# A feed-forward or output tile beside attention: one group of sixteen score pairs instead of two groups of eight

## The chip, the cores and the metric

The kernel runs on one core of a Trainium2 chip. The metric is the device time of one execution in microseconds (us), of which less is better. Numbers for a stretch come from one profiled execution.

## What is computed

A transformer block on x of shape [1, 2048, 512] in float32: 32 heads of 16 for attention, a SwiGLU feed-forward layer of width 1792, and shifts, scales and gates from a condition vector c.

```python
mod = (silu(c) @ w_mod).reshape(c.shape[0], 6, 1, -1)
sa, ca, ga, sb, cb, gb = (mod[:, 0], ..., mod[:, 5])
h = layernorm(x) * (1 + ca) + sa
q, k, v = split(h @ wqkv)                       # 32 heads of 16
p = softmax(einsum("bhqd,bhkd->bhqk", q, k) * 16 ** -0.5)
x = x + ga * (merge(p @ v) @ wo)
h = layernorm(x) * (1 + cb) + sb
x = x + gb * ((silu(h @ w_gate) * (h @ w_up)) @ w_down)
```

## The kernel before

The 2048 queries are cut into four chunks of 512. Attention goes by **units**: 32 of them, each four heads of one chunk. A unit has 16 **steps**, one for each tile of 128 keys; a step has four **pairs**, one for each head. So there are 512 steps and 2048 pairs, and `done` counts pairs.

A pair is two matmuls on TensorE (PE), one in the upper and one in the lower half of the rows of its array, so that they run at the same time, each streaming 512 columns:
- the **score** (`score`, L571): keys by queries of one head, into one of the PSUM banks that `bank` hands out in turn. ScalarE (ACT) reads it and writes its exponential into a tile `pt` (L573).
- the **maximum** (`max_one`, L523): the scores of a unit 20 steps ahead, from whose row maxima the exponent's shift comes. VectorE (DVE) reduces it (L525). Its bank comes from `four`.

A score must wait until ACT has read the score that had its bank before; a maximum likewise for DVE.

The **value products** (`pv_step`, L586) multiply the exponentials of a step with the values. A half of a step is four matmuls, one for each head, in four column strips of the array, over all its 128 rows; float32, so each goes through twice, 256 columns each time. They may be made for steps that end 4 or more pairs before the last pair issued (`4 * halves[0][0] + 8 <= done`), so after each block of them four exponential tiles stay unread.

Attention of the next chunk runs together with the dense layers of the chunk that it has left. In `plain` sections it runs alone: windows of three pairs (`WIN`), then a few halves of value products; scores rotate through three banks (4, 5, 6). In `filled` groups eight pairs are interleaved with twelve **slots** of a dense tile, then come up to six halves of value products (four in the steady state). A slot is two matmuls with 64 of the tile's 128 contracted rows each, one in each half of the array, into the two banks of the tile (3 and 6, `FBANKS`). `accumulate` makes the 24 slots of a tile: phase 0 gives one output the upper and the other the lower rows, phase 1 swaps them. Maxima then have banks 0, 1, 2, scores only 4 and 5, and value products 7. How many slots follow each pair is a table:

```python
TWO = (0, 3, 2, 2, 2, 2, 1, 0)
DOWN = (0, 3, 3, 0, 3, 3, 0, 0)
```

A tile of the gate and up projections, or of the output projection, took two groups of `TWO`, so that a block of value products stood between its phases. A tile of the down projection has 12 slots in all, takes one group of `DOWN`, and changes phase inside the group (`trade=True`): an empty instruction on ACT waits for the last matmuls of phase 0, and the first ones of phase 1 wait for it, so that the row halves do not write a bank at the same time.

All engines' orders are written out by the program (`manual_schedule`); PE and ACT work through theirs in order. What a group has left to do for its tile (tanh, products, additions) is in `posts` and `behind`, what a unit has left (its denominators, `out_a` to `out_c`) in `due`. Row maxima are turned by `max_rows` with three small matmul forms on PE in `plain` sections and by `max_turned` with DVE and a small ACT instruction (L563) in `filled` ones.

Of the kernel before, what the change touches and what calls it, by code (L numbers as in the profile page):

```python
# [11 lines left out]
F32 = mybir.dt.float32  # L12
# [9 lines left out]
P = 128  # L22
# [8 lines left out]
CW = S // NC  # L31
# [8 lines left out]
LEAD = 21  # L40
# [2 lines left out]
HALVES = (2, 1, 1, 2)  # L43
ORDER = (0, 2, 1, 3)
UG = 16 * NG
PTS = 13
FBANKS = (3, 6)
KEEP = 7
REST = 24
NORM = 9  # L50
STARTS = (147, 275, 403)
TWO = (0, 3, 2, 2, 2, 2, 1, 0)
DOWN = (0, 3, 3, 0, 3, 3, 0, 0)
ALONE = {TWO: (0, 4, 0, 4, 0, 4, 0, 0), DOWN: (0, 6, 0, 0, 0, 6, 0, 0)}


# [5 lines left out]
def take(it, k):  # L62
    run(islice(it, k))
# [40 lines left out]
def block_kernel(ctx, tc, x, wqkv, wo, w_gate, w_up, w_down, c, w_mod, out):  # L104
    nc = tc.nc
# [23 lines left out]
    one = const.tile([P, 1], F32, name="one")  # L129
# [8 lines left out]
    o_dr = dram.tile([NC, NG, P, CW], F32, name="o_dr")  # L138
# [353 lines left out]
    pb = ctx.enter_context(tc.tile_pool(name="pb", bufs=2, reuse_waits="tile"))  # L492
    kop[1] = pb.tile([P, 2, S], F32R, name="kop1", bufs=1)
    pf = None
    qop, mx, pts, pv, o_, due, res = {}, {}, {}, {}, {}, {}, {}
    posts, behind = [], []
    n = 16 * NU
    last = NC - 1
# [66 lines left out]
    def score(i, h):  # L565
        u, kt = divmod(i, 16)
        rows = slice(64 * (h % 2), 64 * (h % 2) + KR + 2)
        p_ = pb.tile([P, CW], F32, name="pt_", tag="pt", bufs=PTS)
        pts.setdefault(i, {})[h] = p_
        sp = bank("st_")  # L570
        nc.tensor.matmul(sp, kop[u % 3][rows, h // 2, kt * P:(kt + 1) * P], qop[u][rows, h // 2, :],  # L571
                         start=True, stop=True)
        nc.scalar.activation(p_, sp, AF.Exp, scale=SCALE)  # L573
# [35 lines left out]

    def out_c(u, eng, mul, o, rb):  # L610
        ci, g = divmod(u, NG)
        on = pf.tile([P, CW], F32, name="on", tag="on", bufs=1)
        mul.tensor_mul(on, o, rb)  # L613
        eng.dma_start(o_dr[ci, g], on)

    def at(i, f):
        due.setdefault(i, []).append(f)
# [13 lines left out]
    def tile_mid():  # L631
        return pf.tile([P, 2, CW], F32R, name="mid", tag="mid", bufs=3)

    def tmp(name):
        return pf.tile([P, CW], F32, name=name, tag="tmp", bufs=4)
# [177 lines left out]
    def add_o(ch, t0, outs, late):  # L813
        if ch.mv is None:
            ch.mv = pf.tile([P, 4, 2], F32, name="mv2", tag="mv2", bufs=1)
            ch.rs = pf.tile([P, 4], F32, name="rs", tag="rs", bufs=1)
            ch.rs2 = pf.tile([P, 2, 4], F32, name="rs2", tag="rs2", bufs=1)
        for e in range(2):
            t = t0 + e
            nc.vector.tensor_add(ch.x2[:, t, :], outs[e], ch.x2[:, t, :])  # L820

        def sums(t):
            st = pf.tile([P, 6], F32, name="stt", tag="stt", bufs=2)
            nc.vector.bn_stats(st, ch.x2[:, t, :])
            nc.vector.bn_aggr(ch.mv[:, t, :], st)

        def minus_mean(t):
            nc.scalar.activation(tmp("sq"), ch.x2[:, t, :], AF.Identity, scale=-1.0 / D,
                                 accum_out=ch.mv[:, t, 0:1])

        def squares(t):
            nc.scalar.activation(tmp("sq"), ch.x2[:, t, :], AF.Square, bias=ch.mv[:, t, 0:1],  # L832
                                 accum_out=ch.mv[:, t, 1:2])

        if late:
            turns = (1, 2, 2, 3) if t0 == 0 else (1, 2, 3, 4)
            works = ((minus_mean, t0), (squares, t0), (minus_mean, t0 + 1), (squares, t0 + 1))
            behind.extend([k, lambda f=f, t=t: f(t)] for k, (f, t) in zip(turns, works))
        else:
            for e in range(2):  # L840
                sums(t0 + e)

    def out_pair(ch, t0, outs, halves):
        return accumulate(outs, lambda e, a, k: ch.oT[a][:, k, (t0 + e) * P:(t0 + e + 1) * P],
                          lambda b, k: ch.wo[k // 2][:, b, k % 2, :], NK,
                          lambda: posts.append(lambda: add_o(ch, t0, outs, True)), halves)

    def out_terms(ch, t, pt, ks):
        for k in ks:
# [1 line left out]
                nc.tensor.matmul(pt, ch.oT[a][:, k, t * P:(t + 1) * P], ch.wo[k // 2][:, b, k % 2, :],  # L851
                                 start=(k == 0 and a == b == 0), stop=(k == NK - 1 and a == 1))

    def gate_up(ch, f, outs, halves):
        ch.load_gu(f + ch.ahead)
        if f == 0:
            ch.load_wd(0)
        ch.mid[f] = mid = tile_mid()

        def after():  # L860
            th = tmp("th")
            nc.scalar.activation(th, outs[0], AF.Tanh, scale=0.5)  # L862

            def later():
                q = tmp("q")
                nc.vector.scalar_tensor_tensor(q, th, 1.0, outs[0], op0=ALU.add, op1=ALU.mult)  # L866
                m32 = tmp("m32")
                nc.vector.tensor_mul(m32, outs[1], q)  # L868
                slow = halves or (ch.ci, f) == (last - 1, NF - 2)
                (nc.gpsimd.tensor_copy if slow else nc.scalar.copy)(mid[:, 0, :], m32)  # L870
                (nc.gpsimd if slow else nc.vector).tensor_sub(mid[:, 1, :], m32, mid[:, 0, :].bitcast(F32))  # L871
            posts.append(later)

        w = ch.w.pop(f)
        return accumulate(outs, lambda e, a, k: w[:, 2 * e + a, k, :], lambda b, k: ch.hT[b][:, k, :], NK, after,
                          halves)

    def down(ch, m, t0, outs, halves):
        def later():
# [98 lines left out]
    halves = [(i, half) for i in range(n) for half in range(2)]  # L978
    done, ended, owed = 0, 0, 0
# [16 lines left out]
    for i in range(-LEAD, -1):  # L996
# [7 lines left out]
        if i == -2:  # L1004
            four, work = three, bank
# [11 lines left out]
    def pvs(most, by_halves):  # L1017

        nonlocal owed
        if by_halves:  # L1020
            most, owed = most + owed, 0
        while most and halves and 4 * halves[0][0] + 8 <= done:
            i, half = halves.pop(0)
            pv_step(i, half)
            most -= 1
            if i % 16 == 15 and half:
                close_unit(i // 16, done // 4 - 1)
                if by_halves:
                    break
        if by_halves and most and halves and 4 * halves[0][0] + 8 <= done:  # L1030
            owed = most

    def turns_behind():
        for b in list(behind):
            b[0] -= 1
            if not b[0]:
                b[1]()
                behind.remove(b)

    def end_steps():  # L1040
        nonlocal ended
        while ended < done // 4:
            after(ended - 1)
            ended += 1

    def plain(steps, tails=()):

        nonlocal four, bank, beside
        beside = False
        assert steps % WIN == 0 and done % 4 == 0  # L1050
        four, bank = Turn(0, 3, 1, 2), Turn(4, 5, 6)
        for w in range(4 * steps // WIN):
            for _ in range(WIN):
                pair_of()
            if w < len(tails) and tails[w]:
                tails[w](four())
            pvs((HALVES[(w - 2) % 4] if done > 8 else 0) + (w == 4 * steps // WIN - 1), True)
            turns_behind()
            end_steps()

    def filled(places, work):

        nonlocal four, bank, beside
        beside = True
        four, bank = three, Turn(4, 5)
        if done >= 4 * n - 4 * (LEAD - 1):
            places, bank = ALONE.get(places, places), Turn(4, 5, 0, 1, 2)
        for r in range(len(places)):
            pair_of()
            take(work, places[r])  # L1070
            if r % 4 == 3:
                end_steps()
        hook()
        pvs(6, False)
        turns_behind()

    def two_of(u):
        return [kop[u % 3][:, e, :].rearrange("p (k c) -> p k c", k=NK) for e in range(2)]
# [9 lines left out]
    outs = [banks[b] for b in FBANKS]  # L1088
    pvs(3, False)
    for ci in range(last):  # L1090
        plain(STARTS[ci] - done // 4)
        ch = chunks[ci]
        for t0 in (0, 2):
            work = out_pair(ch, t0, outs, True)
            filled(TWO, work)
            filled(TWO, work)
        behind.append([4, lambda: scaled(ch)])
        tails = [lambda tp, k=k: ch.turned(tp, k) for k in range(NK)]
        plain(NORM, [None] * NORM + tails[:3])
        plain(WIN, tails[3:])  # L1100
        if ci == last - 1:
            plain(REST)
        for _ in range(len(ch.jobs) - (KEEP if ci == last - 1 else 0)):
            job, args = ch.jobs.pop(0)
            if args == (NF // FG - 1, 0):
                plain(WIN)
            work = job(ch, *args, outs, True)
            for places in (TWO, TWO) if job is gate_up else (DOWN,):
                filled(places, work)
    chunks[last - 1].load_gu(NF - 2)  # L1110
    filled((0,) * 4, iter(()))

# [2 lines left out]
    turns = chain([2, 3, 2, 0, 1, 2, 0], cycle([1, 3, 2, 0]))  # L1115
# [19 lines left out]
    ch, chp = chunks[last], chunks[last - 1]  # L1135
# [4 lines left out]
    on = out_b(NU - 1, nc.scalar, *res[NU - 1])  # L1140
    on = out_r(NU - 1, nc.scalar, *on)
# [48 lines left out]
```

## Time and profile before

| | |
|---|---|
| median of 3 runs | 1829.33 us (1827.03 to 1829.35) |
| the profiled execution | 1826.86 us, of which its span 1825.0 us |
| PE matmuls busy | 1816.3 us (100% of the span) |
| PE weight loads busy | 1202.5 us (66%) |
| DVE busy | 1521.2 us (83%) |
| ACT busy | 1248.0 us (68%) |
| GpSimd (POOL) busy | 459.9 us (25%) |

Matmuls that run in different parts of the array overlap, and their ends are modelled, so PE's 100% says that it hardly ever stood with nothing issued, not that no time can be taken out. The start times of successive matmuls tell more than the busy time.

### The profile page before, as it was taken

The numbers are of one execution on the slowest core, as the hardware profiler recorded it, in microseconds if no ns is written. First come the engines' busy times: TensorE is split into PE (matmuls) and PEld (weight loads), VectorE is DVE, ScalarE is ACT, GpSimd is POOL, SyncE is SP. The second block draws the span as 40 slices with busy tenths as digits, with TensorE's granted clock in tenths as the row PEclk, the third lists the DMA queues.
The fourth block names the chain that finished last, engine by engine and source line by source line (L and its number), as shares of the span: only waits on it lengthen the run. The fifth ranks groups of instructions, "written<-read, shape, count | busy, mean of one in ns | idle before, by whom it ended". The sixth has DMA issues, their size and how long they took to land.

```text
span 1825.0 us, 40961 instructions
## 1 busy us (share of the span) xinstructions
PE 1816.3 (100%) x16904; PEld 1202.5 (66%) x16904; DVE 1521.2 (83%) x2554; ACT 1248.0 (68%) x2358; POOL 459.9 (25%) x538
## 2 busy tenths in 40 slices
PE   9999999999999999999999999999999999999999
PEld 7876444444465777776565777776564577777887
DVE  5578999999999888888999888889999988832544
ACT  4223888888888766777888767767888876673211
POOL 3612544556223111111123111111113011131200
PEclk9999999999999999999999999999999999999999
DMA  9883876667845444453544554444643536333742
GB/s 307 288 232 138 203 199 172 179 167 199 207 81 125 103 122 143 115 149 70 145 110 105 141 125 118 122 118 91 161 80 57 116 90 157 134 123 120 279 167 108
DMA packets 80486, 267.62 MB, mean 147 GB/s; under 512 B 19604, under 2 KB 24212, under 8 KB 59620
## 3 DMA queue, kind: packets, MB, share of 16 engines
q1 hardware_dynamic: 61324, 179.71, 34.0%
q0 software_dynamic: 18288, 84.49, 19.5%
q8 instruction: 133, 2.18, 0.5%
q10 hardware_dynamic: 688, 0.80, 0.1%
q14 instruction: 53, 0.43, 0.1%
HBM read 201.85 MB, written 62.13 MB: 145 GB/s over the span
## 4 chain that ended last, share of the span: by engine, by line
PE 83%; DVE 14%; ACT 1%; DMA 0%; issue 0%; SPq 0%; DVEq 0%
PE bank L586 21%; PE bank L789 20%; PE bank L571 14%; DVE mx L525 14%; PE bank L523 11%; PE bank L808 8%; PE bank L213 7%; PE bank L851 1%; PE bank L772 0%; DMA wm_ab<-in_w_mod 0%; PE bank L165 0%; ACT sq L832 0%; DVE v_flat L882 0%; PE bank L537 0%; SPq L261 0%
## 5 line engine op out<-in xcount | busy, mean ns | idle before, releaser
L525 DVE TENSOR_REDUCE mx<-bank 128x1 f32<-128x512 f32 x2048 | 1273.3, 681 | 111.0 <-PE bank L523 63.7
L571 PE MATMUL bank<-qop,kop 50*128 50x512 f32 x2048 | 729.7, 426 | 0.4 <-ACT pt__16494 L573 0.2
L523 PE MATMUL bank<-kop,qop 48*128 48x512 f32 x2048 | 724.6, 425 | 0.3
L571 PEld LDWEIGHTS bank<-qop,kop 50*128 50x128 f32 x2048 | 343.1, 184 | 168.9 <-issue 49.8
L523 PEld LDWEIGHTS bank<-kop,qop 48*128 48x128 f32 x2048 | 342.8, 184 | 106.2 <-DVE mx L525 62.1
L789 PE MATMUL bank<-act,wgu 64*128 64x512 f32 x1872 | 303.5, 392 | 0.0
L789 PEld LDWEIGHTS bank<-act,wgu 64*128 64x128 f32 x1872 | 199.4, 187 | 22.5
L613 POOL TENSOR_TENSOR on<-o,rb 128x512 f32<-128x512 f32 x31 | 39.9, 1286 | 507.8 <-DMA rb<-d_dr 359.0
L789 PE MATMUL bank<-wd,mid 64*128 64x512 f32 x912 | 131.6, 391 | 0.0
L870 POOL CAST mid<-m 128x512 fp32r<-128x512 f32 x40 | 24.4, 609 | 380.5 <-DVE m L868 273.7
L789 PEld LDWEIGHTS bank<-wd,mid 64*128 64x128 f32 x912 | 92.2, 186 | 11.2
L213 PE MATMUL bank<-hT,wqs 128*128 128x512 f32 x384 | 94.4, 397 | 0.4 <-DVE wqs L353 0.4
L866 DVE SCALAR_TENSOR_TENSOR q<-th,bank 128x512 f32<-128x512 f32 x56 | 38.3, 683 | 54.2 <-ACT th L862 54.2
L213 PEld LDWEIGHTS bank<-hT,wqs 128*128 128x128 f32 x384 | 70.6, 188 | 19.1 <-issue 3.2
L862 ACT ACTIVATE th<-bank 128x512 f32<-128x512 f32 x56 | 33.2, 594 | 57.9 <-PE bank L808 57.9
L882 DVE TENSOR_TENSOR x<-bank,x 128x512 f32<-128x512 f32 x84 | 53.9, 685 | 16.1 <-PE bank L789 16.1
L868 DVE TENSOR_TENSOR m<-bank,q 128x512 f32<-128x512 f32 x56 | 38.7, 692 | 21.7 <-PE bank L808 19.7
L871 POOL TENSOR_TENSOR mid<-m,mid 128x512 fp32r<-128x512 f32 x40 | 51.7, 1292 | 3.3
L808 PE MATMUL bank<-wd,mid 128*128 128x512 f32 x216 | 51.3, 393 | 0.0
L213 PE MATMUL bank<-wqs,hT 128*128 128x512 f32 x192 | 48.0, 398 | 0.0
L789 PE MATMUL bank<-wgu,act 64*128 64x512 f32 x288 | 47.6, 392 | 0.0
L808 PEld LDWEIGHTS bank<-wd,mid 128*128 128x128 f32 x216 | 40.4, 188 | 8.9
(6300 smaller groups left out, 5137.3 us busy)
## 6 DMA issues: line engine op xcount, KB each, us to landing
wgu<-gu_dr SPq DMA_DIRECT2D x48, 1024.0 KB
wd<-wd_dr SPq DMA_DIRECT2D x28, 1024.0 KB
kop<-kd SPq DMA_DIRECT2D x33, 768.0 KB
kop<-kd POOLq DMA_DIRECT2D x29, 768.0 KB, 8.8
gu_dr<-wgu POOLq DMA_DIRECT2D x14, 1024.0 KB, 13.6
kd<-prt SPq DMA_DIRECT2D x16, 512.0 KB
qd<-prt SPq DMA_DIRECT2D x16, 512.0 KB
kop<-gu_dr SPq DMA_DIRECT2D x8, 1024.0 KB
```

Source lines behind the costliest of these rows:

```text
L213: nc.tensor.matmul(pt, lhs(a, k), rhs(b, k), start=(n == 0), stop=(n == 3 * nk - 1))
L523: nc.tensor.matmul(pm, qop[u][rows, s, qt * P:(qt + 1) * P], kop[u % 3][rows, s, kc * CW:(kc + 1) * CW], start=True, stop=True)
L525: nc.vector.tensor_reduce(mx[u][:, b, s, qt, kc:kc + 1], pm, op=ALU.max, axis=AX.X)
L571: nc.tensor.matmul(sp, kop[u % 3][rows, h // 2, kt * P:(kt + 1) * P], qop[u][rows, h // 2, :], start=True, stop=True)
L586: nc.tensor.matmul(pv[u][32 * h:32 * h + 32, cols], v_flat[:, e0:e0 + 32], p_[h][:, cols], start=(kt == 0 and half == 0), stop=(kt == 15), ...
L613: mul.tensor_mul(on, o, rb)
L789: mm = nc.tensor.matmul(outs[e], lhs(e, a, k)[rows], rhs(b, k)[rows], start=(ph == 0 and j == 0), stop=(j == z and (ph == 1 or trade)), sk ...
L808: nc.tensor.matmul(outs[e], lhs(e, a, k), rhs(b, k), start=(j == 0), stop=(j == z))
L866: nc.vector.scalar_tensor_tensor(q, th, 1.0, outs[0], op0=ALU.add, op1=ALU.mult)
L868: nc.vector.tensor_mul(m32, outs[1], q)
L871: (nc.gpsimd if slow else nc.vector).tensor_sub(mid[:, 1, :], m32, mid[:, 0, :].bitcast(F32))
L882: nc.vector.tensor_add(ch.x2[:, t, :], outs[e], ch.x2[:, t, :])
```

## The change

A tile of the gate and up projections or of the output projection now runs as one group of sixteen pairs and 24 slots by a new table `FOUR`, with its phase change inside the group, and one block of up to ten halves of value products behind it. A tile that would start in the last step of a unit, or too near the end of the maxima, still takes two groups of `TWO`. Sixteen new exponentials beside four unread ones need 20 tiles instead of 13: 15 of the old kind for heads 0 to 2, and 5 in another pool (`pu`) for head 3. Room for them comes from the descriptor memory of GpSimd's transfers (8192 bytes a partition) and from the tile `on`, whose product now goes into `rb`. Six of the steps that ran plain in the third chunk run later in it, ahead of gate and up tile 7.

```diff
-PTS = 13
+PTS = 5
...
-REST = 24
+REST = 18
...
+FOUR = (0, 2, 2, 2, 1, 2, 0, 3, 0, 2, 2, 2, 2, 2, 2, 0)
...
-        p_ = pb.tile([P, CW], F32, name="pt_", tag="pt", bufs=PTS)
+        place = (pb, "pt", 3 * PTS) if pf is None or h < 3 else (pf, "pu", PTS)
+        p_ = place[0].tile([P, CW], F32, name=place[1] + "_", tag=place[1], bufs=place[2])
...
-        on = pf.tile([P, CW], F32, name="on", tag="on", bufs=1)
-        mul.tensor_mul(on, o, rb)
-        eng.dma_start(o_dr[ci, g], on)
+        mul.tensor_mul(rb, o, rb)
+        eng.dma_start(o_dr[ci, g], rb)
...
-            turns = (1, 2, 2, 3) if t0 == 0 else (1, 2, 3, 4)
+            turns = (1, 1, 2, 2) if t0 == 0 else (1, 2, 3, 4)
...
-        pvs(6, False)
+        pvs(len(places) // 2 + 2, False)
         turns_behind()
+
+    def filled_tile(job, ch, arg):
+        one = done // 4 % 16 != 15 and done + 16 <= 4 * n - 4 * (LEAD - 1)
+        work = job(ch, arg, outs, True, one)
+        for places in (FOUR,) if one else (TWO, TWO):
+            filled(places, work)
...
-            work = out_pair(ch, t0, outs, True)
-            filled(TWO, work)
-            filled(TWO, work)
+            filled_tile(out_pair, ch, t0)
...
-            work = job(ch, *args, outs, True)
-            for places in (TWO, TWO) if job is gate_up else (DOWN,):
-                filled(places, work)
+            if ci == last - 1 and args == (7,):
+                plain(24 - REST)
+            if job is gate_up:
+                filled_tile(job, ch, *args)
+            else:
+                filled(DOWN, job(ch, *args, outs, True))
...
-    nc = _bacc.Bacc("TRN2", target_bir_lowering=False, num_devices=1)
+    nc = _bacc.Bacc("TRN2", target_bir_lowering=False, num_devices=1, dynamic_dma_scratch_size=8192)
```

`out_pair` and `gate_up` hand the flag `one` to `accumulate` as `trade`.

How PE's rows move is seen at one gate and up tile. Scores are those into bank4 and bank5, maxima those into bank0 to bank2, slots are two rows into bank3 and bank6. At the tile's start, before:

```order
L571 MATMUL bank4_67<-qop_5957,kop2_1508 128x512
L523 MATMUL bank0_63<-kop0_88,qop_6581 128x512
L571 MATMUL bank5_68<-qop_5957,kop2_1508 128x512
L523 MATMUL bank1_64<-kop0_88,qop_6581 128x512
L789 MATMUL bank3_66<-act0_1608,wgu_7137 128x512
L789 MATMUL bank6_69<-act0_1608,wgu_7137 128x512
L789 MATMUL bank3_66<-act1_1609,wgu_7137 128x512
L789 MATMUL bank6_69<-act1_1609,wgu_7137 128x512
L789 MATMUL bank3_66<-act0_1608,wgu_7137 128x512
L789 MATMUL bank6_69<-act0_1608,wgu_7137 128x512
L523 MATMUL bank2_65<-kop0_88,qop_6581 128x512
L571 MATMUL bank4_67<-qop_5957,kop2_1508 128x512
```

The same place now (the lines are numbered one or two higher):

```order
L573 MATMUL bank4_67<-qop_5949,kop2_1508 128x512
L524 MATMUL bank0_63<-kop0_88,qop_6574 128x512
L573 MATMUL bank5_68<-qop_5949,kop2_1508 128x512
L524 MATMUL bank1_64<-kop0_88,qop_6574 128x512
L790 MATMUL bank3_66<-act0_1608,wgu_7131 128x512
L790 MATMUL bank6_69<-act0_1608,wgu_7131 128x512
L790 MATMUL bank3_66<-act1_1609,wgu_7131 128x512
L790 MATMUL bank6_69<-act1_1609,wgu_7131 128x512
L524 MATMUL bank2_65<-kop0_88,qop_6574 128x512
L573 MATMUL bank4_67<-qop_5949,kop2_1508 128x512
```

The second score of bank 4 now stands behind two slots instead of three. Further on, from the sixth pair (pair 5, counted from 0) to the eighth, before:

```order
L571 MATMUL bank5_68<-qop_5957,kop2_1508 128x512
L523 MATMUL bank2_65<-kop0_88,qop_6581 128x512
L789 MATMUL bank3_66<-act0_1608,wgu_7137 128x512
L789 MATMUL bank6_69<-act0_1608,wgu_7137 128x512
L789 MATMUL bank3_66<-act1_1609,wgu_7137 128x512
L789 MATMUL bank6_69<-act1_1609,wgu_7137 128x512
L523 MATMUL bank0_63<-kop0_88,qop_6581 128x512
L571 MATMUL bank4_67<-qop_5957,kop2_1508 128x512
L789 MATMUL bank3_66<-act0_1608,wgu_7137 128x512
L789 MATMUL bank6_69<-act0_1608,wgu_7137 128x512
L523 MATMUL bank1_64<-kop0_88,qop_6581 128x512
L571 MATMUL bank5_68<-qop_5957,kop2_1508 128x512
```

From the sixth to the eighth pair now:

```order
L573 MATMUL bank5_68<-qop_5949,kop2_1508 128x512
L524 MATMUL bank2_65<-kop0_88,qop_6574 128x512
L790 MATMUL bank3_66<-act1_1609,wgu_7131 128x512
L790 MATMUL bank6_69<-act1_1609,wgu_7131 128x512
L790 MATMUL bank3_66<-act0_1608,wgu_7131 128x512
L790 MATMUL bank6_69<-act0_1608,wgu_7131 128x512
L524 MATMUL bank0_63<-kop0_88,qop_6574 128x512
L573 MATMUL bank4_67<-qop_5949,kop2_1508 128x512
L524 MATMUL bank1_64<-kop0_88,qop_6574 128x512
L573 MATMUL bank5_68<-qop_5949,kop2_1508 128x512
```

Two slots and one score now stand between the two scores of bank 5, where three slots and one score stood. Behind the eighth pair, before:

```order
L523 MATMUL bank1_64<-kop0_88,qop_6581 128x512
L571 MATMUL bank5_68<-qop_5957,kop2_1508 128x512
L586 MATMUL bank7_70<-pt__7433,v_flat_89 32x256
L586 MATMUL bank7_70<-pt__7461,v_flat_89 32x256
L586 MATMUL bank7_70<-pt__7444,v_flat_89 32x256
L586 MATMUL bank7_70<-pt__7466,v_flat_89 32x256
```

And now:

```order
L573 MATMUL bank5_68<-qop_5949,kop2_1508 128x512
L790 MATMUL bank3_66<-act0_1608,wgu_7131 128x512
L790 MATMUL bank6_69<-act0_1608,wgu_7131 128x512
L790 MATMUL bank3_66<-act1_1609,wgu_7131 128x512
L790 MATMUL bank6_69<-act1_1609,wgu_7131 128x512
L790 MATMUL bank3_66<-act0_1608,wgu_7131 128x512
L790 MATMUL bank6_69<-act0_1608,wgu_7131 128x512
L573 MATMUL bank4_67<-qop_5949,kop2_1508 128x512
L524 MATMUL bank2_65<-kop0_88,qop_6574 128x512
L573 MATMUL bank5_68<-qop_5949,kop2_1508 128x512
L524 MATMUL bank0_63<-kop0_88,qop_6574 128x512
L790 MATMUL bank6_69<-act0_1608,wgu_7131 128x512
```

The block of value products that stood here has moved behind the sixteenth pair; three slots, then the pairs 8 and 9, then the first slot of phase 1 stand in its place. In the whole program 36 tiles run so, and 72 groups of eight have become 36 of sixteen; 46 groups of eight pairs with maxima are left, and ten near the end whose maxima run out or are done are as before.

## Rows read from the trace of the kernel before

**Rows 1.** The page's span and busy times (its part 1).

```profile
span 1825.0 us, 40961 instructions
PE 1816.3 (100%) x16904; PEld 1202.5 (66%) x16904; DVE 1521.2 (83%) x2554; ACT 1248.0 (68%) x2358; POOL 459.9 (25%) x538
```

**Rows 2.** The chain that ended last, shares of the span by line (part 4).

```profile
PE bank L586 21%; PE bank L789 20%; PE bank L571 14%; DVE mx L525 14%; PE bank L523 11%; PE bank L808 8%; PE bank L213 7%; PE bank L851 1%; PE bank L772 0%; DMA wm_ab<-in_w_mod 0%; PE bank L165 0%; ACT sq L832 0%; DVE v_flat L882 0%; PE bank L537 0%; SPq L261 0%
```

**Rows 3.** Timeline of PE, one group of TWO: start us, us, engine, what.

```profile
654.89 0.50 PE L571 MATMUL bank<-qop,kop 50*128 50x512 f32 x1
...
655.23 0.39 PE L571 MATMUL bank<-qop,kop 50*128 50x512 f32 x1
...
655.46 0.87 PE L789 MATMUL bank<-act,wgu 64*128 64x512 f32 x6
...
656.17 0.40 PE L571 MATMUL bank<-qop,kop 50*128 50x512 f32 x1
...
658.25 0.39 PE L571 MATMUL bank<-qop,kop 50*128 50x512 f32 x1
...
659.45 0.40 PE L571 MATMUL bank<-qop,kop 50*128 50x512 f32 x1
659.78 0.40 PE L586 MATMUL bank<-pt__7609,v_flat 128*32 128x256 f32 x1
...
660.02 0.38 PE L586 MATMUL bank<-pt__7609,v_flat 128*32 128x256 f32 x1
...
661.31 0.38 PE L586 MATMUL bank<-pt__7666,v_flat 128*32 128x256 f32 x1
...
661.64 0.50 PE L571 MATMUL bank<-qop,kop 50*128 50x512 f32 x1
```

**Rows 4.** Timeline of ACT in the same group.

```profile
655.42 0.60 ACT L573 ACTIVATE pt__7666<-bank 128x512 f32<-128x512 f32 x1 [1.17 <-PE bank L523]
...
658.68 0.60 ACT L573 ACTIVATE pt__7714<-bank 128x512 f32<-128x512 f32 x1
659.17 0.21 ACT L563 ACTIVATE parts<-m 128x16 fp32r<-128x16 f32 x1
```

**Rows 5.** Timeline of PE's weight loads, the same group.

```profile
656.07 0.18 PEld L571 LDWEIGHTS bank<-qop,kop 50*128 50x128 f32 x1
...
659.33 0.18 PEld L571 LDWEIGHTS bank<-qop,kop 50*128 50x128 f32 x1
```

**Rows 6.** Windows: that group's pairs, its value products, a DOWN group's pairs.

```profile
core 0: us, PE busy (x) PEld busy (x) DVE busy (x) ACT busy (x) POOL busy (x), PEclk, DMA share, GB/s
654.89:659.78 4.89, 4.89 (x45) 4.34 (x41) 4.65 (x9) 3.96 (x8) 2.22 (x3) 1.00 0.61 245
659.78:661.64 1.86, 1.86 (x34) 0.93 (x33) 1.17 (x4) 0.71 (x2) 0.00 (x0) 1.00 0.00 0
627.79:632.73 4.94, 4.94 (x45) 3.87 (x42) 4.49 (x8) 3.50 (x7) 1.90 (x2) 1.00 0.72 100
```

**Rows 7.** Weight load of pair 4's score in that DOWN group.

```profile
630.18 0.18 PEld L571 LDWEIGHTS bank<-qop,kop 50*128 50x128 f32 x1 [0.21 <-ACT pt__7335 L573]
```

**Rows 8.** Timeline of ACT in the DOWN group: the exponential of pair 2.

```profile
629.54 0.60 ACT L573 ACTIVATE pt__7335<-bank 128x512 f32<-128x512 f32 x1
```

**Rows 9.** The chain in order of time, a plain section: start us, us, what.

```profile
358.02 26.93 DVE mx L525 x46
```

**Rows 10.** Timeline of PE in a plain section, around `max_rows`.

```profile
436.56 0.27 PE L536 MATMUL bank<-ident,nm 128*16 128x128 f32 x1
...
437.10 0.49 PE L523 MATMUL bank<-kop,qop 48*128 48x512 f32 x1
```

**Rows 11.** The page's software DMA queue: packets, MB, share of 16 engines.

```profile
q0 software_dynamic: 18288, 84.49, 19.5%
```

More of the change, by code (lines that the diff above doesn't have):

```diff
@@ L841, in add_o, with out_pair @@
                 sums(t0 + e)
-    def out_pair(ch, t0, outs, halves):
+    def out_pair(ch, t0, outs, halves, trade=False):
         return accumulate(outs, lambda e, a, k: ch.oT[a][:, k, (t0 + e) * P:(t0 + e + 1) * P],
                           lambda b, k: ch.wo[k // 2][:, b, k % 2, :], NK,
-                          lambda: posts.append(lambda: add_o(ch, t0, outs, True)), halves)
+                          lambda: posts.append(lambda: add_o(ch, t0, outs, True)), halves, trade=trade)
     def out_terms(ch, t, pt, ks):
@@ L852, in out_terms, with gate_up @@
                                  start=(k == 0 and a == b == 0), stop=(k == NK - 1 and a == 1))
-    def gate_up(ch, f, outs, halves):
+    def gate_up(ch, f, outs, halves, trade=False):
         ch.load_gu(f + ch.ahead)
@@ L875, in gate_up @@
         return accumulate(outs, lambda e, a, k: w[:, 2 * e + a, k, :], lambda b, k: ch.hT[b][:, k, :], NK, after,
-                          halves)
+                          halves, trade=trade)
     def down(ch, m, t0, outs, halves):
```

## The prediction, made before the changed kernel ran

> **What bounds the kernel now.** I read the page's first part, then the chain, then single groups. PE has matmuls under way nearly all the time and DVE is next [rows 1]. The chain is PE's nearly everywhere: the value products L586 hold 21%, the dense tiles L789 and L808 28%, scores and maxima (L571, L523) 25%; DVE's reductions L525 hold 14% [rows 2]. Those 14% lie in plain sections, where one reduction follows the other: 46 in 26.93 us, 0.585 us each [rows 9]. In filled groups PE leads, and only what shortens PE's own order there shortens the kernel.
>
> So I took one group apart by start times [rows 3]. From its first slot (655.46) to the score of its last pair (659.45) stand 17 units, a unit being a pair or a slot: 3.99 us, so 0.235 us a unit. Twenty units would be 4.70 us, but the pairs' stretch takes 4.89 [rows 6]: the second pair comes 0.34 us after the first (654.89 to 655.23), and the first value product 0.33 us after the last pair (659.45 to 659.78), where 0.235 would do. That is 0.2 us for going into and out of the two-halves form. Inside the block of value products successive sets start 0.215 us apart (660.02 to 661.31 is six of them, 1.29 us); eight would be 1.72 us, the block takes 1.86 [rows 6], 0.14 more. One border between the two forms and back therefore costs 0.34 us of PE's time.
>
> The second thing to see is how near the scores are to their two banks. Pair 5's score starts at 658.25 [rows 3], its exponential at 658.68 and ends 0.60 later at 659.28 [rows 4]; only then, at 659.33, is the weight load of pair 7's score let go [rows 5], and the score starts at 659.45 [rows 3]. The cycle of a score bank is 0.43 + 0.60 + 0.05 + 0.12 = 1.20 us. Between these two scores stand one other pair and three slots, five units or 1.175 us with their own. So TWO leaves almost nothing. In a DOWN group the same is seen as a wait: the exponential of pair 2 ends at 629.54 + 0.60 = 630.14 [rows 8], and pair 4's load stands 0.21 us for it until 630.18 [rows 7]; that group's pairs take 4.94 us [rows 6].
>
> **The change part by part.** *Borders.* Each of 36 tiles loses one border. Sixteen pairs, 24 slots and 16 sets without any wait would take 40 x 0.235 + 0.20 + 16 x 0.215 + 0.14 = 13.18 us against 2 x (4.89 + 1.86) = 13.50: by the borders alone 0.34 us a tile, and 36 x 0.34 = 12.2 us for the kernel.
>
> *Score banks.* FOUR still gives scores two banks, and two scores of one bank are 2 + (slots behind the first) + (slots behind the second) units apart. TWO and DOWN never go below five but for the start. FOUR does so three times. First, pair 2: it stands behind two slots, not three. In the old group it started 1.28 us after the group (654.89 to 656.17 [rows 3]), and its load was already let go only after the first exponential (655.42 + 0.60 = 656.02; 656.07 [rows 4, 5]). It cannot start earlier, so the missing slot turns into a wait of 0.235 us. Second, pairs 5 and 7: two slots and then none between, four units, 0.94 us where 1.20 are needed: a wait of 0.26 us. What is queued behind that load on PE is all of the tile, since PE's order is fixed. Third, pairs 8 and 10: again 0.94 us, up to 0.26. Here I reckon differently. The scores of pairs 2, 7 and 10 go through the same half of the rows (odd heads), that of pair 8 through the other. A score held back stops its own half, and the other one goes on as far as the next rows in order are loaded. Pair 8 then runs up to 0.235 us ahead of the half that is late, and its exponential is done in time for pair 10. I take 0 for the third wait and 0.26 for its bound, 0.235 + 0.26 for the first two, and nothing for their bound below (waits that the two halves hide altogether). Sum: 0.50 us a tile.
>
> *Phase change.* It now happens inside the group as in DOWN, with two pairs between. DOWN's stretch is 0.05 us longer than TWO's [rows 6]; the held load of [rows 7] is enough to explain that, so 0, and at most 36 x 0.05 = 1.8 us.
>
> *DVE.* Sixteen reductions at 0.585 us are 9.4 us [rows 9]; the pairs' stretch is 9.6 us without waits and 10.1 with them, and DVE has the block of value products (3.6 us) for the tile's two products. Three banks let it fall two behind. I cost it at nothing; without scores' waits it would have hardly any slack, which is a rival below.
>
> *Exponential tiles.* Four unread and sixteen new ones fill the 20 exactly; all tiles that a group takes were read in the block before it, so ACT waits for none. Cost 0.
>
> *The rest.* Six plain steps move within the third chunk; as many pairs run plain as before. One turn of maxima falls into a filled group instead of a plain one: PE loses the 0.54 us from 436.56 to 437.10 [rows 10], ACT gains a 0.21 us instruction [rows 4]. I take -0.5 us. The product in `rb` makes the next load of `rb` wait for a transfer to DRAM; the next one comes a unit later, 64 pairs or 64 x 0.585 = 37 us in a plain section [rows 9], which hides it. Less descriptor memory could make GpSimd's transfers wait for room; their queue moved 18288 packets in the whole span and kept the engines 19.5% busy [rows 11], and the keys it loads are those of the third unit on. I take 0; were it to wait longer than two such units, 75 us, a unit's first score would be late next.
>
> *Sum.* Per tile -0.34 + 0.50 = +0.16 us; 36 x 0.16 = 5.8; less 0.5: +5.3 us. On the profiled execution (1826.86, span 1825.0 [rows 1] and 1.86 around it) that is 1832.2. It lies 2.5 us under the median of the runs shown, so for the median I say 1829.3 + 5.3 = 1834.6 us.
>
> **The rivals.** *The waits do not count.* If the two halves of the array, or slots issued ahead, hide them, the borders' gain stays: -12.2 - 0.5, 1816.6 us. Place: pairs 2 and 7; it decides from waits under 0.34 us a tile in sum. For it: a wait of one half costs only if the other cannot catch up. Against it: the load rows let go exactly at the exponential's end, in DOWN with PE's load queue idle. By the Trainium skill (Perfetto Trace Analysis, Matmuls under Optimizing Tensor Performance), matmul groups should rotate through PSUM banks, so that ScalarE's evacuation of one overlaps the next group's matmuls; two banks in turn do that, and by the rule the 12 us would come out. The trace agrees that they overlap, and shows with 1.20 us a cycle that two banks suffice only at five units and more.
>
> *Half of them.* Pair 2's wait counts and pair 7's is made good, or the other way round: -0.34 + 0.25 = -0.09 a tile, -3.2 - 0.5, 1825.6 us.
>
> *All three, and the phase change.* 0.50 + 0.26 + 0.05 - 0.34 = +0.47 a tile, +17 - 0.5, 1845.7 us. For it: pair 9 stands directly behind pair 8, and two exponentials close together push the second.
>
> *DVE becomes the bound.* Without score waits, 10 maxima fall into the first 5.0 us of a group; at 0.585 each they need 5.9, and two may be owed; then a wait up to 0.1 us a tile remains, 1817 to 1820 us. It goes with the first rival.
>
> **How the numbers follow.** A measurement of this kernel can tell about 0.2%, 3.7 us, from no change. The forecast's case, +0.06 to +0.26 a tile, or +2 to +9 us, has 0.62; some 0.1 of that lies under 3.7 us. The first rival with DVE's has 0.15, half of the waits 0.11 (at the edge between faster and same), all three 0.12. Faster: 0.15 + 0.04 = 0.19. Same: 0.10 + 0.07 = 0.17. Slower: 0.52 + 0.12 = 0.64. The range reaches from the half case to halfway to the worst, 1825 to 1842 us; it leaves out the first rival and the worst. The forecast's own range is 1831 to 1838.
>
> **What would show it.** In a group of sixteen the pairs should take 10.1 us (9.6 if the first rival is right, 10.4 the worst), the value products 3.58. Score loads of pairs 2 and 7 should begin 0.05 us after the exponential two scores before ends, and slots behind them late in one half. If the pairs' stretch is under 9.7, step two of my sum is wrong. If the stretch is right and the total is not, look at plain sections and at GpSimd's queue, which I costed at nothing.

## The result, and the profile after

| | before | after |
|---|---|---|
| median of 6 runs each | 1827.87 us (1826.51 to 1829.35) | 1835.36 us (1834.34 to 1837.49) |
| ratio, with its 95% interval | | 1.0042 (1.0029 to 1.0055) |
| the profiled execution | 1826.86 us, span 1825.0 | 1835.68 us, span 1833.9 |

The change made the kernel 7.5 us slower where 5.3 were forecast. 1834.6 us was said and 1835.4 came, but that these lie so near is partly luck: the forecast started from 1829.3, which is 1.5 us above the median of all six runs before. The page of the changed kernel first, its span, busy times and the chain by line; they answer to [rows 1, 2].

```profile
span 1833.9 us, 41022 instructions
PE 1823.2 (99%) x16898; PEld 1198.0 (65%) x16898; DVE 1512.2 (82%) x2556; ACT 1247.0 (68%) x2357; POOL 460.7 (25%) x538
...
PE bank L588 26%; PE bank L790 19%; PE bank L573 18%; PE bank L524 15%; PE bank L809 8%; PE bank L214 7%; DVE mx L526 2%; PE bank L852 1%; DMA wm_ab<-in_w_mod 0%; PE bank L773 0%; PE bank L166 0%; ACT sq L833 0%; DMA qop<-mr 0%; PE bank L538 0%; DVE v_flat L883 0%
```

The busy times hardly move, and they name no cause. The chain's share of DVE falls from 14% to 2%, and that is no cause either: DVE is as busy as before. The faster kernel `e1_spaced` below has 14% again, with the same plain sections; I take it that reductions and matmuls end so close together there that the chain goes once through the one and once through the other, which no run here shows by itself. What tells is one group of sixteen. Two windows of it, its pairs and its value products, answer to [rows 6].

```profile
core 0: us, PE busy (x) PEld busy (x) DVE busy (x) ACT busy (x) POOL busy (x), PEclk, DMA share, GB/s
683.93:694.09 10.16, 10.16 (x85) 7.92 (x81) 9.66 (x16) 8.54 (x16) 0.00 (x0) 1.00 0.91 256
694.09:697.68 3.59, 3.59 (x67) 1.98 (x65) 2.04 (x4) 1.02 (x3) 1.28 (x2) 1.00 0.70 242
```

Forecast were 10.1 and 3.58 us. Over all 36 groups the medians, taken from the starts of their first and last rows, are 10.17 and 3.59. Two groups of eight took 2 x (4.89 + 1.86) = 13.50 [rows 6]; this one takes 13.75. The clock is granted in full in both windows. Next, the weight loads of scores in that group, from its third pair (pair 2) to its eleventh (pair 10), and ahead of the last the load of that pair's maximum. In brackets stands how long the load queue stood idle, and whose end ended that.

```profile
685.11 0.18 PEld L573 LDWEIGHTS bank<-qop,kop 50*128 50x128 f32 x1 [0.19 <-ACT pt__8025 L575]
685.69 0.18 PEld L573 LDWEIGHTS bank<-qop,kop 50*128 50x128 f32 x1
686.29 0.18 PEld L573 LDWEIGHTS bank<-qop,kop 50*128 50x128 f32 x1
686.99 0.18 PEld L573 LDWEIGHTS bank<-qop,kop 50*128 50x128 f32 x1 [0.20 <-ACT pu__8050 L575]
687.57 0.18 PEld L573 LDWEIGHTS bank<-qop,kop 50*128 50x128 f32 x1
688.17 0.18 PEld L573 LDWEIGHTS bank<-qop,kop 50*128 50x128 f32 x1 [0.19 <-ACT pt__8064 L575]
688.91 0.18 PEld L573 LDWEIGHTS bank<-qop,kop 50*128 50x128 f32 x1
689.40 0.18 PEld L573 LDWEIGHTS bank<-qop,kop 50*128 50x128 f32 x1 [0.24 <-ACT pu__8080 L575]
...
689.98 0.18 PEld L524 LDWEIGHTS bank<-kop,qop 48*128 48x128 f32 x1
690.13 0.18 PEld L573 LDWEIGHTS bank<-qop,kop 50*128 50x128 f32 x1
```

And ACT's exponentials that these loads name, of pairs 0, 3, 5 and 7, and that of pair 8.

```profile
684.46 0.60 ACT L575 ACTIVATE pt__8025<-bank 128x512 f32<-128x512 f32 x1 [1.41 <-PE bank L524]
...
686.34 0.60 ACT L575 ACTIVATE pu__8050<-bank 128x512 f32<-128x512 f32 x1
...
687.52 0.60 ACT L575 ACTIVATE pt__8064<-bank 128x512 f32<-128x512 f32 x1
...
688.75 0.59 ACT L575 ACTIVATE pu__8080<-bank 128x512 f32<-128x512 f32 x1
689.48 0.60 ACT L575 ACTIVATE pt__8090<-bank 128x512 f32<-128x512 f32 x1
```

Read the two views side by side. The exponential of pair 0 ends at 685.06, and pair 2's load goes at 685.11, 0.05 later: 1.18 us after the group's start, exactly as in the old group (654.89 to 656.07, [rows 3, 5]), although one slot fewer stands ahead of it. The missing slot has become a wait. Pair 5's exponential ends at 688.12 and pair 7's load goes at 688.17. Pairs 2 and 7 are the two that were forecast. Pair 10's load (690.13) has no bracket, and yet it waited: pair 8's exponential ended at 689.48 + 0.60 = 690.08, again 0.05 earlier. The queue was not idle meanwhile, since the maximum's load ran from 689.98 to 690.16. So it is in all 36 groups. Two waits were not named ahead: pair 5 waits for pair 3's exponential (686.94, load 686.99), pair 9 for pair 7's (689.34, load 689.40).

The heads of a step come in the order 0, 2, 1, 3, so pairs 2, 3, 6, 7 and 10 use the odd heads' half of the rows and pairs 0, 1, 4, 5, 8 and 9 the other. Pair 3 follows the late pair 2 in its half; its exponential is late, and pair 5 in the other half waits for it. Pair 9 stands so to pair 7. The lateness of one half is handed to the other through the banks. In between the halves run apart, which the timeline of PE shows where pair 2 is held.

```profile
684.96 0.40 PE L524 MATMUL bank<-kop,qop 48*128 48x512 f32 x1
685.11 0.50 PE L573 MATMUL bank<-qop,kop 50*128 50x512 f32 x1
685.20 0.64 PE L790 MATMUL bank<-act,wgu 64*128 64x512 f32 x3
685.68 0.39 PE L524 MATMUL bank<-kop,qop 48*128 48x512 f32 x1
685.68 0.62 PE L790 MATMUL bank<-act,wgu 64*128 64x512 f32 x2
685.92 0.39 PE L573 MATMUL bank<-qop,kop 50*128 50x512 f32 x1
686.14 0.62 PE L790 MATMUL bank<-act,wgu 64*128 64x512 f32 x3
```

Slots are two matmuls each; runs of three say that one half is a matmul ahead. The Trainium skill (TensorEngine Tiling (Array Packing), Key Properties) says that tiles of the array operate independently and can load weights and multiply in parallel; the trace agrees, but only up to the next shared bank. The rows show the price of a wait, too: pair 2's matmul starts together with its load (both at 685.11), where a load that is free goes 0.23 us ahead of its matmul (pair 3's at 685.69, matmul at 685.92). The wait has used up that lead.

How much each place costs is read from the half of the rows that is behind. Four rows of PE: the maximum of pair 4, score and maximum of pair 8, and the score of pair 10; the maxima and the last score stand 10, 20 and 24 units behind the group's start.

```profile
686.60 0.39 PE L524 MATMUL bank<-kop,qop 48*128 48x512 f32 x1
...
688.98 0.42 PE L573 MATMUL bank<-qop,kop 50*128 50x512 f32 x1
689.20 0.40 PE L524 MATMUL bank<-kop,qop 48*128 48x512 f32 x1
...
690.21 0.42 PE L573 MATMUL bank<-qop,kop 50*128 50x512 f32 x1
```

With 0.235 us a unit and 0.10 for the way into the form they would start at 686.38, 688.73 and 689.67; they are 0.22, 0.47 and 0.54 us late, and the value products 0.56. Over all 36 groups the medians are 0.24, 0.49, 0.55 and 0.57. So the first place costs 0.24 us, the second 0.25, and the third, pairs 9 and 10, the other 0.08. A part of that may be the phase change's: ACT's empty instruction stands in its order directly ahead of pair 8's exponential, which starts 0.50 us after its score (688.98, 689.48; 0.51 on the median of the 36 groups), where those of pairs 3 and 11 to 14 take 0.43.

Place by place, 34 of the 36 tiles can be set against the old kernel's: 13.78 us on the mean against 13.57, +0.216 a tile or 36 x 0.216 = +7.8 us. At the last score the changed kernel is 8.3 us behind. 0.6 us of that arises at one score, pair 320, the first of a unit, in a plain section ahead of any merged tile: PE stands idle until the transfer that brings the row maxima of its unit (`qop<-mr`) has landed. The profiles of e1, e6 and e7 below, with the same tiles and memory, do not have this wait. So 0.6 us is a size below which one profile against another says nothing.

### The profile page after: what moved, and what is told of

It is laid out like the page before. It is cut to its first block, busy times and chain, and to the rows that moved or that the text cites. A ratio compares the mean times of both kernels' runs of the same rounds, so it can differ in the third digit from the quotient of the medians.

```text
span 1833.9 us, 41022 instructions
## 1 busy us (share of the span) xinstructions
PE 1823.2 (99%) x16898; PEld 1198.0 (65%) x16898; DVE 1512.2 (82%) x2556; ACT 1247.0 (68%) x2357; POOL 460.7 (25%) x538
## 4 chain that ended last, share of the span: by engine, by line
PE 95%; DVE 2%; ACT 2%; DMA 1%; SPq 0%; issue 0%; DVEq 0%
PE bank L588 26%; PE bank L790 19%; PE bank L573 18%; PE bank L524 15%; PE bank L809 8%; PE bank L214 7%; DVE mx L526 2%; PE bank L852 1%; DMA wm_ab<-in_w_mod 0%; PE bank L773 0%; PE bank L166 0%; ACT sq L833 0%; DMA qop<-mr 0%; PE bank L538 0%; DVE v_flat L883 0%
## 5 line engine op out<-in xcount | busy, mean ns | idle before, releaser
L573 PE MATMUL bank<-qop,kop 50*128 50x512 f32 x2048 | 747.5, 432 | 1.0 <-DMA qop<-mr 0.4
L524 PEld LDWEIGHTS bank<-kop,qop 48*128 48x128 f32 x2048 | 345.0, 184 | 106.2 <-DVE mx L526 62.7
L790 PE MATMUL bank<-act,wgu 64*128 64x512 f32 x1872 | 319.9, 393 | 0.0
L790 PEld LDWEIGHTS bank<-act,wgu 64*128 64x128 f32 x1872 | 211.8, 187 | 21.2
L614 POOL TENSOR_TENSOR rb<-o,rb 128x512 f32<-128x512 f32 x31 | 39.9, 1286 | 531.5 <-DMA rb<-d_dr 414.1
```

Source lines behind the costliest of these rows:

```text
L524: nc.tensor.matmul(pm, qop[u][rows, s, qt * P:(qt + 1) * P], kop[u % 3][rows, s, kc * CW:(kc + 1) * CW], start=True, stop=True)
L614: mul.tensor_mul(rb, o, rb)
L790: mm = nc.tensor.matmul(outs[e], lhs(e, a, k)[rows], rhs(b, k)[rows], start=(ph == 0 and j == 0), stop=(j == z and (ph == 1 or trade)), sk ...
```

## The experiments

My theory A: two scores of one bank stand too near in `FOUR`, and this eats the border that was saved. Rival B: it is the other parts of the change (moved steps, tiles, `rb`, descriptor memory). Rival C: the phase change inside the group. All ratios are against the kernel before, run beside them (1827.3 to 1827.4 us).

**e1_spaced**: the changed kernel with the 24 slots placed so that two scores of one bank are always five units or more apart, still with two pairs between the phases.

```diff
-FOUR = (0, 2, 2, 2, 1, 2, 0, 3, 0, 2, 2, 2, 2, 2, 2, 0)
+FOUR = (0, 3, 2, 1, 2, 1, 3, 0, 3, 1, 2, 1, 2, 2, 1, 0)
```

> The changed kernel with another table for the sixteen pairs, (0, 3, 2, 1, 2, 1, 3, 0, 3, 1, 2, 1, 2, 2, 1, 0): no two scores of one bank are nearer than five units, the phase change still has two pairs between, all else as changed. Theory A (two score banks, scores of one bank too near): the pairs' stretch of a sixteen falls from 10.17 us to about 9.8 (40 units of 0.235, 0.2 for the border, 0.05 to 0.2 of short waits at five units), so 36 x 0.4 = 14 us less than the changed kernel, 1821 us, 0.4% under the old one. Rival B (the other parts of the change cost the time: descriptor memory, the product in rb, twenty tiles, the moved plain steps): 1835 us as changed, the stretch may fall but the total doesn't follow. Rival C (the phase change inside the group): stretch and total as changed.

1821.95 us (1820.32 to 1825.98, 10 runs), ratio 0.9974 (0.9965 to 0.9983): 0.3% faster than the kernel before, clear of its interval, and faster than the changed one. The same two windows of it:

```profile
680.69:690.41 9.72, 9.72 (x85) 7.44 (x81) 9.32 (x16) 8.10 (x15) 0.00 (x0) 1.00 0.95 266
690.41:694.00 3.59, 3.59 (x67) 1.98 (x65) 2.20 (x4) 1.24 (x3) 1.13 (x2) 1.00 0.65 253
```

The value products take 3.59 as before the edit, the pairs 9.75 on the median against 10.17. Nothing but the places of eight slots differs, and 13.4 us lie between the medians (12.9 when each is set against the kernel before, run beside it). Other places for slots are other places for the maxima and for the phase change too, but loads of maxima stand 62.7 us for DVE in the whole trace of the changed kernel and 62.1 in this one, and no slot is seen to wait for the phase change in either. At most the 0.08 us a tile of the third place, 3 us in all, could be the phase change's. So 10 us or more are theory A's, and the sign of the change hangs on them. Five units are 1.175 us against a bank's cycle of 1.20, so some loads still wait, such as pair 4's; 0.15 us a tile over the 9.60 without waits are left.

```profile
683.07 0.18 PEld L573 LDWEIGHTS bank<-qop,kop 50*128 50x128 f32 x1 [0.21 <-ACT pt__8043 L575]
```

The brackets alone would mislead here. Behind the first pair, 195 loads of scores wait for ACT in the 36 groups, against 132 in the changed kernel, and still the groups are 0.42 us shorter. What counts is the lead that is left: pair 4's matmul starts 0.05 us after its load, and so 0.05 to 0.11 us are left at every held pair, where the changed kernel has 0.00 at pairs 2, 5, 7 and 9 (medians).

```profile
683.12 0.45 PE L573 MATMUL bank<-qop,kop 50*128 50x512 f32 x1
```

**e2_two_groups**: everything of the change except the merged groups.

```diff
-        one = done // 4 % 16 != 15 and done + 16 <= 4 * n - 4 * (LEAD - 1)
+        one = False
```

> The changed kernel with every tile in two groups of eight by the old table; the twenty exponential tiles, the product in rb, the smaller descriptor memory and the moved plain steps stay. Theory A: all of the loss lies in the groups of sixteen, so the old time less the 0.5 us of one turn of maxima, 1827 to 1828 us. Rival B: most of the loss stays, 1832 to 1835 us. Rival C: the old time, as theory A.

1829.94 us (1829.06 to 1833.51, 11 runs), ratio 1.0014 (1.0006 to 1.0023). A miss: some 2.5 us more than the kernel before, where 0 or a gain was expected. 5.4 us lie between it and the changed kernel: most of the loss is in the merged groups, but the rest of the edits holds something too. In the trace three output tiles are each 0.55 to 0.63 us later than before, which pointed to `turns`, retuned for merged groups; e8 and e9 go into that.

**e3_old_closer**: the old kernel with its groups of eight made as tight at pair 2 as `FOUR` is.

```diff
-TWO = (0, 3, 2, 2, 2, 2, 1, 0)
+TWO = (0, 2, 2, 2, 2, 2, 2, 0)
```

> The old kernel with one slot moved from behind the second pair to behind the seventh in its table of eight, (0, 2, 2, 2, 2, 2, 2, 0): one wait of the suspected kind, at the third pair, where the first exponential cannot be done earlier; nothing merged. Theory A: each of the 84 groups with maxima takes about 0.22 us more (0.235 less what the other half catches up), 18 us in all, 1846 us. Rival (one late score is hidden because the other half of the rows runs on): the old 1828 us.

1846.8 us (1845.67 to 1847.44, 4 runs), ratio 1.0105 (1.0089 to 1.012). Theory A works without any merging: one slot moved by a few places in each group costs 19 us. One group's pairs:

```profile
825.99:831.10 5.11, 5.11 (x44) 4.11 (x40) 4.61 (x10) 4.08 (x8) 1.89 (x2) 1.00 0.58 236
```

5.11 against 4.89 [rows 6] is 0.22, where a missing slot should cost 0.235.

**e4_half_exp** and **e5_half_exp_old**: the exponential is taken over the first 256 of 512 columns only, and both halves of the value products read these; half of the exponentials are left out. PE's order is untouched. e4 is the changed kernel, e5 the old one.

```diff
-        nc.scalar.activation(p_, sp, AF.Exp, scale=SCALE)
+        nc.scalar.activation(p_[:, 0:HQ], sp[:, 0:HQ], AF.Exp, scale=SCALE)
...
-            nc.tensor.matmul(pv[u][32 * h:32 * h + 32, cols], v_flat[:, e0:e0 + 32], p_[h][:, cols],
+            nc.tensor.matmul(pv[u][32 * h:32 * h + 32, cols], v_flat[:, e0:e0 + 32], p_[h][:, 0:HQ],
```

> The changed kernel with ACT taking only the first 256 of a score's 512 columns; both halves of the value products then read these columns. It leaves out half of the exponentials, so the second half of each chunk's attention output is not the reference's; matmuls, reductions and their order are as changed. Theory A (a score waits until ACT has read its bank): an exponential falls from 0.60 to about 0.39 us (0.60 less 256 columns at the 0.83 ns that 0.43 us for 512 columns of streaming would give), a bank's cycle from 1.20 to about 0.99, so four units, 0.94, nearly suffice: stretch of the sixteen 9.65 instead of 10.17, 36 x 0.5 = 18 us under the changed kernel, 1817 us. If the loss has nothing to do with ACT's reading: 1835 us or a little under.

> The old kernel with the same halving, as the base for the run before it; it leaves out the same half of the exponentials. Theory A: the old groups have hardly a score wait to lose (some 0.02 to 0.05 us a group), and plain sections go by DVE: 1824 to 1828 us. The changed kernel should then stand 8 to 12 us under this one, where with whole exponentials it stood 7.5 us above; without theory A it would still stand 5 to 8 us above.

e4 took 1811.09 us (ratio 0.9913, 0.9898 to 0.9928), e5 1819.21 (0.9958, 0.9943 to 0.9973; 4 runs each). An exponential of e4, and the pairs of a group of its sixteen:

```profile
680.21 0.38 ACT L575 ACTIVATE pt__8030<-bank 128x256 f32<-128x256 f32 x1
```

```profile
679.40:689.02 9.62, 9.62 (x84) 8.52 (x81) 9.32 (x16) 5.52 (x16) 0.00 (x0) 1.00 0.97 266
```

With 0.22 us off the bank's cycle, `FOUR` itself runs without its waits: behind the first pair no load of a score waits for ACT in any of the 36 groups. A group takes 9.66 us on the median, 9.65 expected, and the changed kernel lies 8.1 us under the old one instead of 7.5 over it. So the waits are on ACT's reading of the score banks, and the borders' gain is really there. The miss is e5: I thought the old kernel would gain little, and it gained 8.2 us. Its trace is 7.6 us shorter than that of the kernel before: 3.6 in the 118 groups of eight (4.93 to 4.90 us on the mean), 1.5 in the eleven windows of six pairs in plain sections, and 2.0 ahead of the first pair and from the last group on, where hardly an exponential is taken and the traces of all runs differ by more than 3 us. So about 5 us are the exponentials'; the rest is not shown to be. What carries the verdict is e4 against e5, where everything but the merging and its companions is alike.

**e6_three_score_banks**: in merged groups, bank 2 is taken from the maxima and given to the scores.

```diff
+        elif places is FOUR:
+            four, bank = Turn(0, 1), Turn(4, 5, 2)
```

> The changed kernel with bank 2 given to the scores in groups of sixteen: three banks for scores and two for maxima, the table as changed. Theory A: the score waits go, but a maximum's bank is now read by DVE with 0.69 us a reduction, 0.6 apart, and a cycle of about 1.3 us against 0.94 to 1.4 between two of one bank, so the waits come back on maxima and are larger: stretch about 10.8, 1857 us. If ACT by itself were too slow for the first ten pairs: the score waits stay and the maxima add theirs, over 1860 us. If neither bank matters: 1835 us.

1862.09 us (2 runs), ratio 1.0191 (1.0171 to 1.0211). The pairs' stretch, two loads of maxima in it, and the row of the view of waits for such loads over the whole execution (total us, times, longest):

```profile
687.80:698.65 10.85, 10.66 (x84) 7.64 (x81) 10.12 (x16) 8.62 (x16) 0.00 (x0) 1.00 0.87 242
```

```profile
689.12 0.18 PEld L524 LDWEIGHTS bank<-kop,qop 48*128 48x128 f32 x1 [0.55 <-DVE mx L526]
...
692.44 0.18 PEld L524 LDWEIGHTS bank<-kop,qop 48*128 48x128 f32 x1 [0.41 <-DVE mx L526]
```

```profile
PEld bank L524 <- DVE mx L526: 121.2, 327, 0.6
```

The wait moved rather than vanished. Behind the first pair no load of a score waits for ACT any more in the 36 groups, where the changed kernel has 132 such waits. So ACT is fast enough for these pairs, and a third bank takes its wait away, although the time, 5 us over the 1857 expected, would fit the rival with the slow ACT as well. In the changed kernel the same row reads:

```profile
PEld bank L524 <- DVE mx L526: 62.7, 183, 0.4
```

144 waits more are four in each of 36 groups: with `FOUR`, two banks are fewer than the maxima can do with. Whether two would do for them with the spaced table of e1 was not run.

**e7_phase_one_pair**: as e1, but with one pair between the last slot of phase 0 and the first of phase 1, for rival C.

```diff
-FOUR = (0, 2, 2, 2, 1, 2, 0, 3, 0, 2, 2, 2, 2, 2, 2, 0)
+FOUR = (0, 3, 2, 1, 2, 1, 3, 1, 2, 1, 2, 1, 2, 2, 1, 0)
```

> The changed kernel with the table (0, 3, 2, 1, 2, 1, 3, 1, 2, 1, 2, 1, 2, 2, 1, 0): scores spaced as in the run e1_spaced, but only one pair instead of two between the last slot of phase 0 and the first of phase 1. Theory A with the phase change as a second, separate wait: the first slot of phase 1 waits about 0.2 us for ACT's empty instruction, stretch 9.92 instead of 9.75, 36 x 0.17 = 6 us over e1_spaced, 1828 us. If the phase change costs nothing at any distance: 1822 us as e1_spaced. If it costs its full price even with two pairs between (rival C): no more than e1_spaced either, since it was paid there already.

1825.47 us (1823.17 to 1828.8, 10 runs), ratio 0.9989 (0.998 to 0.9999): 3.5 over e1 where 6 were expected. A pairs' stretch of it, then the load of the first slot of phase 1, which waits for ACT's empty instruction:

```profile
683.78:693.59 9.81, 9.81 (x84) 7.59 (x80) 9.38 (x16) 8.19 (x15) 0.00 (x0) 1.00 0.92 261
```

```profile
688.66 0.19 PEld L790 LDWEIGHTS bank<-act,wgu 64*128 64x128 f32 x2 [0.31 <-ACTq L799]
```

With one pair between, the phase change costs 0.08 us a group (9.83 against 9.75 on the medians); of a queue's 0.31 us of waiting most is made good. The view of waits has one such load in each group of e7, and none in the changed kernel or in e1, where two pairs stand between.

```profile
PEld bank L790 <- ACTq L799: 11.1, 36, 0.3
```

So C holds up no slot in the changed kernel; what it may do to pair 8's exponential there is 0.08 us a tile at most, and no run separates that.

**e8_two_groups_turns** and **e9_two_groups_turns_rest**: e2 with the old `turns`, then the old `REST` too. What remains new in e9 are tiles, `rb` and descriptor memory.

```diff
-            turns = (1, 1, 2, 2) if t0 == 0 else (1, 2, 3, 4)
+            turns = (1, 2, 2, 3) if t0 == 0 else (1, 2, 3, 4)
...
-REST = 18
+REST = 24
```

> The run e2_two_groups, which lay 2.6 us over the old kernel instead of 0.5 under it, with the old turns (1, 2, 2, 3) for the output tiles' row sums. In its trace the three output tiles lie 0.55, 0.63 and 0.57 us behind the old ones, since two ACT instructions of these sums fall into one block of value products. If that is the cause: 1.7 us less, 1828.2 us. If the loss is spread (exponential tiles, product in rb, descriptor memory): 1829.9 us as before.

> The same with REST back at 24, so that the six plain steps stand where they stood; what is left of the change is the twenty exponential tiles, the product in rb and the descriptor memory. If these cost nothing and the moved steps cost what the turn of maxima was to save: the old 1827.4 us. If the moved steps did save 0.5 us: 0.5 over the run before it. If tiles or memory cost: 1828.5 us or more.

e8: 1828.98 us (11 runs), ratio 1.0015 (1.0006 to 1.0024). e9: 1828.26 (11 runs), 1.0008 (1.0 to 1.0017). By medians `turns` costs 1.0 us in e2, the moved steps 0.7, and 1.0 stays with the three others, but the intervals overlap: only that e2 and e8 are slower than the kernel before is shown by the times, not how their 1 to 3 us divide. The traces say a little more. Behind the moved steps, from pair 1700 to pair 2000, e8 falls 0.8 us further behind the kernel before, e9 0.1. And in e9 the 118 groups of eight take 4.931 us on the mean, against 4.930: tiles, `rb` and memory cost nothing there. Its last score is 2.8 us late, of which 2.2 arise at pairs 320, 538 and 539, ahead of every dense tile, where transfers (row maxima, denominators) land late; e8's trace has 0.2 us of that. Whether the smaller descriptor memory makes such late landings more frequent stays open. `turns` is no loss where the groups are merged, for which it was retuned; there it is within the tiles' +0.216.

## Why the prediction was right, step by step

**Borders (-12.2 us): right.** A border of value products less is worth 0.34 us a tile by its two parts, 0.14 in the block and 0.20 in the pairs' stretch (the sum's own 13.50 - 13.18 gives 0.32). The block came out at 3.59 us for 3.58. The other part is seen only together with what waits are left: the tile comes down to 9.75 + 3.59 = 13.34 us with e1 and to 9.66 + 3.59 = 13.25 with e4, against 13.50 before and 13.18 without any wait. The Trainium skill (TensorEngine Tiling (Array Packing), Key Properties) says that a change of the tiling mode drains the engine, without a figure; the traces agree that going from one form to the other costs time, 0.34 us there and back, and no run shows that it is a drain.

**Score banks (+0.50 us a tile): right in mechanism, a little small in size.** Loads are let go 0.05 us after the exponential, at the pairs named, and moving slots (e1, e3), halving exponentials (e4) or a third bank (e6) takes the waits away or brings them as the cycle of 1.20 us says. The term measures 10.17 - 9.60 = 0.57. The first two places cost 0.24 and 0.25 us where 0.235 and 0.26 were reckoned. What was mis-sized is the third place, put at 0: pair 8's exponential was not done in time for pair 10, whose load waited for it, and pair 9 before it had waited for pair 7's. From pair 8 on 0.08 us were lost, within the 0.26 given as the bound. The sentence that a held score stops its own half alone was too kind, since the banks hand the lateness to pairs 5 and 9.

**Phase change (0): right, to 0.08 us a tile at most.** No slot is seen to wait for it in the changed kernel's trace, and e7 against e1 shows what one that waits costs. What of the third place's 0.08 us is due to the empty instruction ahead of pair 8's exponential stays open. **DVE (0): right.** Loads of maxima stand 62.7 us for DVE in the changed kernel's trace (183 times), 62.1 in the one before (182 times). Without the score waits it comes near, as the rival had it: in e4 31 loads of maxima in the 36 groups wait for DVE, in the changed kernel 4. **Exponential tiles and memory (0): right in the groups, open beside them.** e9 loses nothing in its groups of eight; by its interval 0 to some 3 us are left for late transfers.

**The rest (-0.5 us): wrong in sign, as far as e8 and e9 show.** The moved steps cost +0.7 us by medians, whose intervals overlap, and as much by the traces. The turn of maxima did leave the plain sections (six matmuls of PE fewer, 16898 for 16904), so something costs more than it saves; what, stays open. In the changed kernel's own trace, 8.9 us of longer span less 7.8 in its tiles leave about +1, half of it at pair 320.

So the forecast's +5.3 came out as +7.5: +2 from the tiles (0.216 instead of 0.16 each, 36 x 0.056), and what is left, 0.2, is less than the runs' scatter. "The waits do not count" is refuted by the kernel itself. Its gain comes out in part once two scores of one bank stand five units apart (e1: 5.4 us under the kernel before) or the reading is short enough (e4: 8.1 us under e5), of the 12.2 that the borders are worth.

## What to carry to other kernels

Before slots are placed between matmuls, work out the cycle of one bank from start times: from the matmul's start to its reader's start, the reading, the release, and the load of the next (here 0.43 + 0.60 + 0.05 + 0.12 = 1.20 us); what stands between two uses of a bank must last about that long at every place in the table, at a group's start too. A load that is held takes its matmul's lead first, and what is lost begins where the lead is used up. A merge that saves a border can so turn from a loss of 7.5 us to a gain of 5.4 by the places of eight of 24 slots alone. Do the same for every ring of banks that shares the order, since a bank taken from one to help another (e6) only moves the wait.

## What the runs showed beside that

- The two row halves of the array run on apart by a matmul or so, and a half that is held hands its lateness to the other two or three pairs later, through the bank that they share (loads of pairs 5 and 9, 0.20 and 0.24 us).
- ACT's share of 68% looked like slack, yet halving the exponential's length from 0.60 to 0.38 us gave the old kernel 8.2 us, of which its trace shows about 5 in groups of eight and in plain windows.
- A first slot of phase 1 stood 0.31 us for an empty instruction of ACT (e7), of which the group's stretch showed only 0.08, and e1 has more loads that wait than the changed kernel (195 against 132) in shorter groups: waits of PE's load queue aren't to be added up as lost time.
